# Seven products in the middle layer of two token blocks, with a given order for TensorE

## Chip, cores, metric

One Trainium2 chip, one core. The metric is the device time of one execution in microseconds (us). Every timed run has a state, fast or slow, by its time against the fastest of the same kernel; only fast runs enter a ratio.

## The reference

```python
# q, k, v: (8, 8, 576, 64); w_in: (512, 2048); w_out: (2048, 512); all float32
scores = q @ k.transpose(0, 1, 3, 2) / 8
ret = scores * Dmat                      # gamma_h ** (i - j) for i >= j, else 0
x = (ret @ v).transpose(0, 2, 1, 3).reshape(4608, 512)
h = x @ w_in
out = (h * cos(h)) @ w_out               # (4608, 512) float32
```

## The kernel before

PSUM, in banks, is where TensorE leaves its results; SBUF is where the other tiles stand. The tokens go through in nine blocks of 512, numbered from 0. Attention runs in "sessions" (64x64 matmuls) that end in an x tile `xt`. The middle layer makes h, the cosine and their product g (`gt`) in 16 tiles a block; the last layer multiplies g with `w_out`.

Middle layer, one tile: four matmuls, a cosine on ScalarE from PSUM, a multiply on VectorE (g multiply) from PSUM and SBUF.

```python
def mlp1(self, j, f, ses, prio):
    ...
    for c in range(4):
        inst = e.matmul(bank, WIN[c, f], xt[c], start=(c == 0), stop=(c == 3))   # 512 columns
    self.one("act", ..., e.activation(cb, bank, AF.Sin, bias=CPI))               # cos(h) = sin(h + pi/2)
    self.one("dve", ..., e.tensor_tensor(gt[f], bank, cb, ALU.mult))             # g = h cos(h)
```

Last layer of blocks 1 to 8: a 2x2 block product by seven products instead of eight. VectorE makes the operand sums (S sums, bf16); ScalarE copies a bank out in the middle of an accumulation (a snapshot), because products 1, 6, 7 and 4 accumulate in the same bank A; VectorE combines.

```python
def wino2(self, j, base, span):
    for q in range(2):                          # S1 .. S4: 128x1024 bf16 <- two SBUF inputs
        self.one("dve", 610, lambda e: e.tensor_tensor(sv(i, q), x(), y(), op), ..., port=True, name=f"S{i}_{j}")
    ...
    for n, p in enumerate((1, 2, 6, 5, 7, 3, 4)):
        ...                                     # two tasks of 8 matmuls, 256 columns each
        if p == 1: snap("p1", A)                # ScalarE copies the bank
        elif p == 2: comb(0, 0, Bb, "p1")       # VectorE: PSUM + SBUF -> SBUF, float32
        elif p == 6: snap("u2", A)
        ...
```

The order on every engine comes from a list scheduler that the program runs while it is being built. Operations marked `port` (elementwise work between SBUF tiles on VectorE or GpSimd) are kept apart in its reckoning.

```python
def pick(e):
    for t in ready[e]:
        s = max(free[e], est[t], a)
        if t.port:
            s = max(s, port_free["pool" if e == "dve" else "dve"])
        if t.ni:
            s = max(s, fetched(t))              # a model of instruction fetch, TensorE only
        cand.append((s, t))
    ...
```

GpSimd casts k (`natk`), scales v (`natv`) and most of q (`qnat`), and issues the weight loads.

## Time and profile before

| | before |
|---|---|
| timed, first comparison | 306.41, 306.94, 306.71 fast, 314.08 slow; mean of the fast 306.69 us |
| profiled run | 312.0 us (a slow one), span 310.3 |
| TensorE, VectorE, ScalarE, GpSimd busy | 95, 66, 61, 35% |

### The profile page before, as it was taken

What the parts mean: (1) busy time and instruction counts of PE and PEld (TensorE: products, weight loads), DVE (VectorE), ACT (ScalarE), POOL (GpSimd) and SP (SyncE); (2) the same over time, 40 slices, a digit from 0 to 9 for tenths busy, and PEclk for the clock granted to TensorE, in tenths of its full rate; (3) what the DMA queues carried; (4) which work ended last, traced back from release to release, by engine and by line L of the source; (5) the groups of instructions that cost most, each with busy time, mean ns of one, the idle gap of its engine ahead of it and who ended that gap; (6) DMA issues with size and microseconds to landing.
All of it is one profiled execution on the core that took longest, in us unless ns stands there. A gap on an engine that the chain in (4) does not pass through costs nothing.

```text
span 310.3 us, 10091 instructions
## 1 busy us (share of the span) xinstructions
PE 294.1 (95%) x4274; PEld 214.7 (69%) x4277; DVE 206.3 (66%) x371; ACT 188.3 (61%) x340; POOL 108.9 (35%) x134
## 2 busy tenths in 40 slices
PE   8987999799889999999998799999999999999995
PEld 8866755688778888567855375768656666666684
DVE  3574973475984769898478487775769667666641
ACT  3476843888959775856373566474686665455430
POOL 2261058759517581931362631312741000000000
PEclk9999999999999999999999799999999999999999
DMA  9999999999977999894999749269701100300123
GB/s 172 222 159 206 205 229 217 253 270 219 219 157 189 122 204 285 159 171 109 234 219 247 181 48 235 61 114 195 161 13 72 70 2 0 127 10 2 63 76 136
DMA packets 126397, 46.80 MB, mean 151 GB/s; under 512 B 105104, under 2 KB 122000, under 8 KB 126352
## 3 DMA queue, kind: packets, MB, share of 16 engines
q1 hardware_dynamic: 122128, 41.95, 63.3%
q0 software_dynamic: 4224, 4.19, 8.4%
q8 instruction: 34, 0.56, 0.8%
q14 instruction: 11, 0.09, 0.1%
HBM read 36.70 MB, written 9.44 MB: 149 GB/s over the span
## 4 chain that ended last, share of the span: by engine, by line
PE 87%; DVE 3%; ACT 3%; issue 2%; DMA 2%; POOL 2%; DVEq 0%
PE bk L763 39%; PE bk L886 32%; PE bk L800 4%; PE bk L418 2%; DMA stgq<-in_q_dram 2%; PE bk L661 2%; PE bk L652 2%; PE bk L634 2%; PE st L643 2%; PE bk L575 2%; DVE gt L774 1%; PE bk L593 1%; DVE pt L723 1%; POOL win L743 1%; POOL wout L747 1%
## 5 line engine op out<-in xcount | busy, mean ns | idle before, releaser
L774 DVE TENSOR_TENSOR gt<-bk,cb 128x256 bf16<-128x256 f32 (+1 forms) x192 | 103.7, 555 | 59.5 <-ACT cb L771 52.9
L763 PE MATMUL bk<-xt,win 128*128 128x256 bf16 (+1 forms) x768 | 140.1, 327 | 2.3 <-issue 1.3
L771 ACT ACTIVATE cb<-bk,cpi 128x256 bf16<-128x256 f32 (+1 forms) x192 | 108.4, 585 | 55.6 <-PE bk L763 54.0
L763 PEld LDWEIGHTS bk<-xt,win 128*128 128x128 bf16 x768 | 72.9, 98 | 44.0 <-issue 2.3
L512 POOL TENSOR_TENSOR natv<-stgv,wv 128x512 bf16<-128x512 f32 x38 | 41.3, 1097 | 36.1 <-DMA stgv<-in_v_dram 23.3
L477 POOL CAST natk<-stgk 128x512 bf16<-128x512 f32 x36 | 22.0, 626 | 62.0 <-DMA stgk<-in_k_dram 34.6
L557 POOL TENSOR_TENSOR qnat<-stgq,wq 128x512 bf16<-128x512 f32 x36 | 38.6, 1092 | 13.5 <-DMA stgq<-in_q_dram 5.9
L723 DVE TENSOR_TENSOR pt<-bk,tri 128x512 bf16<-128x512 f32 (+1 forms) x46 | 29.6, 683 | 14.8 <-PE st L643 12.8
L476 ACT ACTIVATE sbd<-st 128x512 bf16<-128x512 f32 x32 | 19.3, 603 | 22.6 <-PE st L643 22.4
L886 PE MATMUL bk<-wout,s 128*128 128x256 bf16 x256 | 32.2, 273 | 0.0
L886 PE MATMUL bk<-tw,s 128*128 128x256 bf16 x256 | 31.6, 273 | 0.5 <-DVE s L847 0.5
L886 PE MATMUL bk<-wout,gt 128*128 128x256 bf16 x256 | 31.6, 273 | 0.0
L886 PEld LDWEIGHTS bk<-wout,s 128*128 128x128 bf16 x256 | 24.7, 98 | 6.6
L886 PEld LDWEIGHTS bk<-tw,s 128*128 128x128 bf16 x256 | 24.6, 98 | 6.1 <-DVE s L847 0.8
L886 PEld LDWEIGHTS bk<-wout,gt 128*128 128x128 bf16 x256 | 24.7, 98 | 4.6 <-DVE pt L723 0.2
L476 ACT ACTIVATE sn<-bk 128x512 f32<-128x512 f32 x24 | 14.4, 604 | 18.7 <-PE bk L886 18.7
L476 ACT ACTIVATE xt<-bk 128x512 bf16<-128x512 f32 x36 | 23.1, 694 | 0.3 <-PE bk L661 0.2
L898 DVE TENSOR_TENSOR os<-bk,sn 128x512 f32<-128x512 f32 x24 | 16.4, 685 | 8.2 <-PE bk L886 8.2
L886 PE MATMUL bk<-tw,gt 128*128 128x256 bf16 x128 | 17.3, 282 | 0.0
L886 PEld LDWEIGHTS bk<-tw,gt 128*128 128x128 bf16 x128 | 12.9, 101 | 4.2 <-issue 0.6
L418 PE MATMUL bk<-one 128*128 128x128 bf16 x181 | 14.3, 244 | 1.1 <-DVE lq L441 1.1
L800 PE MATMUL bk<-wout,gt 128*128 128x512 bf16 x61 | 14.8, 379 | 0.2
(63 smaller groups left out, 230.7 us busy)
## 6 DMA issues: line engine op xcount, KB each, us to landing
stgk<-in_k_dram SPq DMA_DIRECT2D x32, 256.0 KB, 5.0
stgv<-in_v_dram SPq DMA_DIRECT2D x32, 256.0 KB, 5.4
out_dram<-os SPq DMA_DIRECT2D x15, 512.0 KB, 3.5
stgq<-in_q_dram SPq DMA_DIRECT2D x12, 512.0 KB, 7.0
stgq<-in_q_dram SPq DMA_DIRECT2D x8, 256.0 KB, 4.9
win<-in_moe_w_in_dram POOLq DMA_DIRECT2D x4, 512.0 KB, 7.6
wout<-in_moe_w_out_dram POOLq DMA_DIRECT2D x4, 512.0 KB, 14.7
out_dram<-os SPq DMA_DIRECT2D x6, 256.0 KB, 3.5
```

The lines of the kernel that those rows point to most:

```text
L418: inst = e.matmul(ap(self.at(self.wb), 512, 0, 128, 0, [1, 128]), self.ONE.ap(), self.ONE.ap(), start=True, stop=True, skip_group_check=True)
L476: return self.one(eng, dur, lambda e: e.activation(dst(), src(), AF.Copy), r=r, w=w, **kw)
L477: return self.one(eng, dur, lambda e: e.tensor_copy(dst(), src()), r=r, w=w, port=True, **kw)
L512: self.one(ve, vd, lambda e, b2=b2: e.tensor_tensor(ap(self.at(t["natv"]), 1024, 0, 128, 512 * b2, [D, H], [1, D]), ap(self.at(t["stgv"]), ...
L557: self.one("dve" if fast else "pool", 620 if fast else 990, lambda e, t=t, y=y: e.tensor_tensor(ap(self.at(t["qnat"]), 1024, 0, 128, y * 5 ...
L723: self.one("dve", 610, lambda e, hp=hp: e.tensor_tensor(ap(self.at(pt), 1024, p0, n, 512 * hp, [64, 8], [1, 64]), ap(self.at(sc[hp]), 512, ...
L763: inst = e.matmul(ap(self.at(bk), 512, 0, 128, 0, [1, n]), ap(self.WIN, 4 * DFF, 0, 128, c * DFF + 128 * f, [1, 128]), ap(self.at(xt), 204 ...
L771: self.one("act", 70 + n, lambda e: e.activation(ap(self.at(cb), TB, 0, 128, 0, [1, n]), ap(self.at(bk), 512, 0, 128, 0, [1, n]), AF.Sin, ...
L774: self.one("dve", 75 + n / 0.96, lambda e: e.tensor_tensor(ap(self.at(gt), NF * TB, 0, 128, f * TB + 256 * h0, [1, n]), ap(self.at(bk), 51 ...
L800: inst = e.matmul(self.at(bk).ap(), ap(self.at(gt), NF * TB, 0, 128, f * TB + 256 * half + 128 * tt, [1, 128]), ap(self.WOUT, NF * DM, 0, ...
L886: inst = e.matmul(ap(self.at(bank), 512, 0, 128, 256 * tt, [1, 256]), l(f, tt), rr(f), start=(first and f == 0 and tt == 0), stop=True, sk ...
L898: self.one("dve", 610, lambda e: e.tensor_tensor(view(h, c), ap(self.at(bank), 512, 0, 128, 0, [256, 2], [1, 256]), ap(self.at(sn[name]), ...
```

## The change

Its intent: save TensorE's streaming in the middle layer of blocks 7 and 8 by seven products there too; give TensorE's order as a list found beforehand, with the other engines scheduled around it; make the start shorter.

```diff
+    SEVEN = 7
+    ORDER = [int(x) for x in """2 0 1 3 4 10 5 6 ... 409 410 411""".split()]   # 412 TensorE tasks (cut)
+    FIRST = [(0, "v", 0), (1, "q", 1)]
-    NOXBAR = set(range(7))
+    NOXBAR = set(range(8))
@@ Prog.add: also an engine's own earlier reads are waited for
-            deps += [d for d in readers if d.eng != eng or d.sem or sem]
+            deps += [d for d in readers if d.eng != "pe" or eng != "pe"]
@@ Graph.run: fetch model and priority rule for TensorE go
+                if e == "pe" and t.idx != first:
+                    continue
@@ weight sums, once, 8 of 128x1024 bf16
+    def win_sums(self):
+        ...
+                self.one("pool", 2100, lambda e, dst=dst, x=x, y=y: e.tensor_tensor(dst(), x(), y(), ALU.subtract),
+                         r=r, w=[w], port=True, late=4000)
@@ operand sums of x, 4 of 128x512 bf16 a block
+    def xsums(self, j):
+            self.one("dve", 340, lambda e, ...: e.tensor_tensor(v(i), x(), y(), op), ..., port=True, name=f"X{i}_{j}")
@@ seven products M1 .. M7 for each of 4 groups a block
+    def mlp1w(self, j, g, base, span):
+        for n, p in enumerate((1, 2, 6, 5, 7, 3, 4)):
+            ...                               # 4 matmuls of 256 columns; snapshots on ScalarE, combines on VectorE
+            eng = "dve" if bank else "pool"   # 12 of 16 g multiplies a block on GpSimd, from SBUF
+            self.one(eng, 608 if eng == "dve" else 1000, lambda e: e.tensor_tensor(out(h, n), h_tile, cb, ALU.mult), ...)
@@ graph
+            if j + 1 == self.SEVEN:
+                tiles([X(15), Y(15), X(17), Y(17)])
+                self.win_sums()
+            if not last and j + 1 >= self.SEVEN:
+                self.xsums(j + 1)
+                for g in range(4):
+                    self.mlp1w(j + 1, g, base + PER * g / 4, PER / 4)
... (cut: the filler count, bookkeeping of buffers, the gates of the weight loads)
```

`NOXBAR` names the tiles that TensorE transposes, not a DMA; both traces have 16 DMA transposes, so it changes nothing here. Fillers are matmuls on constants at the start whose result nobody uses.

## The prediction

> **What bounds the kernel now.** I read the page first (busy shares, chain that ended last), then the same chain in order of time, TensorE's waits, busy time by stage, the groups by shape, and last the timeline of the first 25 us.
>
> ```profile
> span 310.3 us, 10091 instructions
> ...
> PE 294.1 (95%) x4274; PEld 214.7 (69%) x4277; DVE 206.3 (66%) x371; ACT 188.3 (61%) x340; POOL 108.9 (35%) x134
> ...
> PE 87%; DVE 3%; ACT 3%; issue 2%; DMA 2%; POOL 2%; DVEq 0%
> ```
>
> TensorE is busy 95% of the span and holds 87% of the last chain; VectorE and ScalarE have a third of the span free. So time is TensorE's own streaming, plus its waits. The chain in order of time gives both streaming rates (start us, us, what):
>
> ```profile
> 11.67 6.10 DMA stgq<-in_q_dram
> 18.07 2.30 POOL win L743 x3
> 20.36 2.22 POOL wout L747 x3
> 22.59 1.08 POOL natv L512
> ...
> 126.15 8.63 PE bk L763 x40
> ...
> 169.47 3.28 issue
> ...
> 293.95 13.12 PE bk L886 x120
> ```
>
> 40 matmuls of 512 columns in 8.63 us are 216 ns each; 120 of 256 columns in 13.12 us are 109 ns each. A middle-layer tile over a whole block (4 x 216) costs 0.86 us, half a product of the last layer (8 x 109) 0.87 us. The first four lines are the start: a query load, then six weight-load issues on GpSimd, then the value scaling that the y session waits for.
>
> TensorE's waits (engine, line, waited for: us, times, longest):
>
> ```profile
> PE st L643 <- issue: 3.3, 1, 3.3
> PE bk L634 <- POOL natv L512: 1.8, 1, 1.8
> PE bk L763 <- issue: 1.3, 1, 1.3
> ...
> PE bk L575 <- DVE gt L774: 1.0, 1, 1.0
> PE bk L763 <- ACT xt L476: 0.8, 1, 0.8
> ```
>
> The largest does not belong to the timed runs, I think. Busy time by stage, around it (PE, PEld, DVE, ACT, POOL, then granted clock, DMA share, GB/s):
>
> ```profile
> 125.00:169.20 44.20, 44.20 (x562) 28.91 (x561) 33.95 (x50) 26.46 (x42) 20.74 (x22) 1.00 0.89 189
> 169.20:177.00 7.80, 4.52 (x79) 2.55 (x70) 3.23 (x6) 3.32 (x6) 3.88 (x5) 0.78 0.93 239
> ```
>
> The stall, and half clock for about 3.4 us behind it, cost about 3.4 + 1.7 = 5.1 us. The profiled execution took 312.0 us, the timed median is 306.71: 5.3 us less. So a timed run probably has neither, and on the profile's axis its TensorE ends at 307.1 - 5.2 = 301.9 us. From 123 us to the end it then has no wait worth naming.
>
> **What the skill says.** "TensorE: Matmul & The Clock Gate", Back-to-back issue gap, gives N/2.4 + 2.5 ns for an isolated warm matmul: 109 and 216 ns for 256 and 512 columns, which is what the chain shows (its lower 131 ns at N=512 with weight loads is not seen here). Same page, What's actually happening: the clock halves after about 3.4 us idle; the 3.3 us stall with clock 0.78 behind it agrees. "Runtime: NRT & Kernel Launch", Instruction fetch mechanics: instructions stream in blocks of 256 by a DMA queue, the crossing "mostly hidden". The page counts 34 instruction packets on one queue, and the two issue waits (1.3 and 3.3 us) look like such fetches come late behind data. "GPSIMD Engine Reference", Elementwise, has GpSimd 1.96 times slower than VectorE at tensor_tensor; here it is less, 1095 against 685 ns for 128x512.
>
> **The change, part by part.**
>
> *Seven products for the middle layer of blocks 7 and 8* (numbered from 0). Removed: 16 tiles of 4 matmuls at 512 columns per block, 64 x 216 ns = 13.8 us. Added: 4 groups x 7 products x 4 matmuls at 256 columns, 112 x 109 ns = 12.2 us. Saved on TensorE: 1.6 us a block, 3.2 us for two, where TensorE sets the time. Around it:
>
> ```profile
> L771 ACT ACTIVATE cb<-bk,cpi 128x512 bf16<-128x512 f32 x96 | 66.1, 688 | 44.6 <-PE bk L763 44.4
> L774 DVE TENSOR_TENSOR gt<-bk,cb 128x512 bf16<-128x512 f32 x96 | 65.2, 689 | 37.0 <-ACT cb L771 33.5 <-PE bk L763 3.0
> ...
> L512 POOL TENSOR_TENSOR natv<-stgv,wv 128x512 bf16<-128x512 f32 x38 | 41.3, 1097 | 36.1 <-DMA stgv<-in_v_dram 23.3 <-PE bk L661 12.3
> ...
> L898 DVE TENSOR_TENSOR os<-bk,sn 128x512 f32<-128x512 f32 x24 | 16.4, 685 | 8.2 <-PE bk L886 8.2
> ...
> L476 ACT ACTIVATE sn<-bk 128x512 f32<-128x512 f32 x24 | 14.4, 604 | 18.7 <-PE bk L886 18.7
> ```
>
> A block's group has 3 snapshots more on ScalarE: 12 x 604 = 7.2 us a block. VectorE's 16 multiplies of 689 ns become 12 combines of 685 and 4 multiplies, so the same, plus 4 operand sums of about 0.4. GpSimd, idle from 240 us on before, takes 12 multiplies a block of about 1.1 us and once eight weight sums of 128x1024, which I estimate at 2.2 us each by doubling its 1097 ns: 44 us in all. A late block has 12.2 us of middle and 12.2 us of last layer on TensorE, 24.4 us; ScalarE's 11.0 + 7.2 + 2.4 = 20.6 us (Sin, snapshots, the last layer's copies) and VectorE's 11.0 + 1.6 + 6.1 + 2.1 = 20.8 us (combines and multiplies, operand sums, the last layer's sums and combines) stay below, at 85%. They fit but have little slack left: bank A is snapshotted between products 1, 6 and 7, and drain 0.2 + copy 0.6 + signal 0.05 us is covered only by two products of 0.44 us between. In most groups the order has those two; in one (block 7, third group) product 6 follows product 1 directly: 0.85 us lost.
>
> *The given order.* TensorE's waits of the 24 to 125 us stretch, from start-to-start times against the usual of each task: 0.9 and 0.3 before the x2/x3 session, 0.9 for xt behind it, 0.4, 0.6 + 0.4 behind the x4 session, 0.7 (a sum S1), 0.3, 0.2, 0.1: 4.9 us, besides the 1.5 of an issue wait at 28 us. In the changed order I measured the same way how much TensorE work lies between each producer and its consumer. It puts output tiles of the last layer between the x2/x3 tasks (-1.2), seven middle tiles before y2/y3 (-0.4) and an earlier last tile before S1 (-0.5). It keeps the xt wait (0.9; the middle layer still follows its session directly), about 0.7 around the x4 session, and gains new ones: 0.45 before session 12/13 (its bank is left by a tile issued 0.87 us before; chain 0.2 + 0.69 + 0.69 + signals), 0.85 as above, some 0.3 in small ones. These come to 3.2 us; before, the same arithmetic gave 2.4 where the trace had 4.9, because engines also queue. I take 4.0. So order: -0.9.
>
> *Start, fillers.* The fillers are not fewer in the built program: 184 against 181, but 29 instead of 71 stand before the first transpose, which before was ready by 4.6 us and ran at 7.5:
>
> ```profile
> 1.13 6.55 PE L418 MATMUL bk<-one 128*128 128x128 bf16 x71 [1.13 <-DVE lq L441]
> 7.51 0.39 PE L575 MATMUL bk<-idn,natk 128*128 128x128 bf16 x4
> ```
>
> The transposed query copy, and the second query's scaling queued behind it on VectorE (10.9 us), come some 2 us earlier, and so does the 11.67 us load in the chain. DMA is busy there, so I count 0.9 us of it at the y session, of which 0.44 goes back: one middle tile fewer stands before that session. Net -0.5.
>
> *Tail.* One product of block 7 now fills a wait near the end, so its store of 512 KB goes out beside the last ones: +0.3.
>
> Sum: -3.2 - 0.9 - 0.5 + 0.3 = -4.3; 306.7 - 4.3 = 302.4 us, 1.4% faster.
>
> **Rivals.** *Nothing is left of the seven products:* copies and combines in chains with no slack give 0.3 us in each of 8 groups back, 2.4 us, and the time is near 305. For it: ScalarE and VectorE at 85%, thin spacing. Against: the order was chosen around just these. *Order pays in full:* waits of 1.5 us in place of 4.9, and 1.6 us at the start, make it 306.7 - 3.2 - 3.4 - 1.6 + 0.3 = 298.8. For it: every wait of before sits at a place that a list can repair. Against: the xt wait and the one after product 1 stand in the new list. *Fetch:* the order rule that looked at instruction fetch is gone and there are about 200 TensorE instructions more; one stall as at 169 us in timed runs would be 3 to 5 us: 306. For it: it happened in the profiled run even with the rule. Against: most dense stretches (sessions) are spaced as before.
>
> **Range and chances.** The spread is +-1.5 from the order, +-1 from the start, +-1.5 from the late blocks, upward also a fetch: 299.0 to 305.8. Faster by over 2% needs under 300.6, a gain of 6.1, which the second rival alone reaches: 0.25. Within 2%: 0.72. Slower: 0.03.
>
> **What would show it.** Middle-layer products at 109 ns each and 24.4 us of them; the first transpose near 4.6 us and the y session near 23 us instead of 23.8; TensorE's waits for ScalarE snapshots and VectorE combines in the last 90 us under 2 us in total; GpSimd busy there. I am wrong if that stretch shows waits of several us, if GpSimd's weight sums are waited for, if issue waits are new, or if the early stretch has lost its waits altogether.

## More of the kernel before

The prediction shows the lines on TensorE. Two more matter later. First, the stages after 228 us (columns: stage, length, busy time and instructions of PE, PEld, DVE, ACT, POOL, then granted clock, DMA share, GB/s):

```profile
228.00:256.00 28.00, 28.00 (x410) 17.76 (x409) 21.86 (x34) 19.63 (x34) 2.08 (x2) 1.00 0.11 40
256.00:300.00 44.00, 43.94 (x338) 30.35 (x337) 29.49 (x45) 20.96 (x32) 0.00 (x0) 1.00 0.13 49
```

TensorE is idle for 0.06 of these 72 us, and GpSimd (fifth pair) has nearly nothing to do. Second, VectorE's S sums of the same stretch (228 to 303 us; line, engine, out<-in, shapes, count | busy us, mean ns | idle before):

```profile
L847 DVE TENSOR_TENSOR s<-s,gt 128x1024 bf16<-128x1024 bf16 x6 | 4.7, 780 | 0.2
L853 DVE TENSOR_TENSOR s<-gt,s 128x1024 bf16<-128x1024 bf16 x6 | 4.1, 687 | 0.1
```

About 690 ns is what such a sum takes when GpSimd is idle; the 780 is taken up again below.

## The result, and the profile after

The changed kernel took 318.46, 317.65 and 316.71 us in fast runs (mean 317.61) and 321.96 in a slow one; it is correct. Ratios here are the mean of one kernel's fast runs over the mean of the other's fast runs of the same rounds, so not quite the ratio of the medians: 317.61 / 306.69 = 1.036, with a 95% interval of 1.031 to 1.040. It is slower by 3.6%, outside the predicted range. The profiled run is a fast one (318.46 us).

From the page of the changed kernel, busy shares and the chain that ended last:

```profile
PE 294.9 (93%) x4376; PEld 223.8 (71%) x4376; DVE 216.4 (68%) x379; ACT 199.2 (63%) x364; POOL 154.7 (49%) x166
...
PE 78%; DVE 7%; ACT 6%; DMA 4%; issue 2%; POOL 2%; POOLq 1%; DVEq 0%
```

TensorE's share of the chain fell from 87 to 78%; VectorE's and ScalarE's rose from 3% each to 7 and 6%. GpSimd's busy time rose by 46 us. TensorE's busy time did not fall, although there is less to stream: part of it ran at half clock. The stages tell where (columns as above):

```profile
169.00:186.00 17.00, 14.98 (x202) 9.04 (x200) 15.14 (x22) 10.18 (x18) 8.45 (x7) 0.90 1.05 232
228.00:256.00 28.00, 24.04 (x416) 17.56 (x415) 21.13 (x28) 16.27 (x31) 15.75 (x11) 0.94 0.11 40
256.00:300.00 44.00, 42.46 (x496) 36.27 (x495) 35.02 (x50) 33.87 (x59) 25.66 (x22) 1.00 0.07 26
```

From 228 to 256 us TensorE is idle for 4 of 28 us and the clock is 0.94, where before it had not a gap. TensorE's waits (engine, line, waited for: us, times, longest):

```profile
PE bk L647 <- DVE gt L787: 3.2, 2, 2.0
PE bk L901 <- DVE s L828: 2.2, 1, 2.2
...
PE bk L901 <- DVE stgq L891: 0.8, 1, 0.8
PE bk L901 <- ACT stgv L489: 0.7, 1, 0.7
```

L647 is a session: it waited 2.0 us at 177 us (2.4 us by start-to-start times, which is the figure used further below) and 1.2 us at 240 us for a bank that VectorE's g multiply was to leave. L901 are the seven products; the largest of their waits is for an operand sum of x. Here is that one, in the timelines of VectorE, GpSimd and TensorE (start us, us, engine, line, out<-in, count):

```profile
243.48 0.82 DVE L992 TENSOR_TENSOR s<-gt 128x1024 bf16<-128x1024 bf16 x1
244.22 3.52 DVE L828 TENSOR_TENSOR s<-xt 128x512 bf16<-128x512 bf16 x2
247.66 0.41 DVE L828 TENSOR_TENSOR s<-s,xt 128x512 bf16<-128x512 bf16 x1
...
243.70 2.58 POOL L809 TENSOR_TENSOR stgk<-win,stgk 128x1024 bf16<-128x1024 bf16 x1
246.24 1.22 POOL L525 TENSOR_TENSOR natv<-stgv,wv 128x512 bf16<-128x512 f32 x1
...
248.13 1.21 PE L901 MATMUL bk<-s,stgk 128*128 128x256 bf16 x6 [2.17 <-DVE s L828]
```

Two x sums took 3.52 us together. The third, with GpSimd idle, took 0.41. The first ended 0.28 us after GpSimd's weight sum had ended, the second 0.28 us after GpSimd's scaling of v, and TensorE's next product waited 2.17 us. Behind this wait, and behind that at 177 us, the granted clock was half for 3.4 us (columns of the stages):

```profile
180.20:183.60 3.40, 3.40 (x88) 2.61 (x74) 3.40 (x5) 2.84 (x5) 1.24 (x1) 0.50 1.16 152
248.40:251.80 3.40, 3.40 (x19) 2.44 (x17) 2.19 (x5) 1.60 (x3) 0.00 (x0) 0.50 0.02 5
```

A product's four matmuls took 0.85 us there instead of 0.44, so each of these stretches cost about 1.7 us. The holding shows as well in the means of VectorE's sums from 228 to 303 us (columns as above):

```profile
L998 DVE TENSOR_TENSOR s<-gt,s 128x1024 bf16<-128x1024 bf16 x5 | 6.8, 1367 | 0.1
L828 DVE TENSOR_TENSOR s<-xt 128x512 bf16<-128x512 bf16 x4 | 5.8, 1484 | 0.7 <-ACT xt L489 0.7
```

### What TensorE lost, by stage

To compare kernels with different work and order, I gave each of TensorE's tasks (a tile, half a product, a session) the shortest start-to-start time that its kind has in any of the traces (the lowest tenth, where there are over 30 of a kind). The sum is the work; what a stretch took above its work is lost: waits, half clock and the fill at the start. Stages end at the amount of work that the kernel before had done at 53, 125, 186 and 228 us. This is my reckoning from the traces, one profiled run per kernel. Stretches of half clock come early in some runs and not in others (list_only at 71.6 us, later_dve at 21.0 and 72.2 us), so in the first two columns differences of 1 or 2 us say little. All values are us; the rows below the second belong to the experiments.

| kernel | work | to 53 | 53-125 | 125-186 | 186-228 | after 228 | TensorE ends |
|---|---|---|---|---|---|---|---|
| before | 270.8 | 23.0 | 6.7 | 5.6 | 0.4 | 0.6 | 307.1 |
| changed | 267.6 | 24.5 | 5.8 | 4.1 | 0.8 | 10.0 | 312.8 |
| list_only | 270.8 | 24.1 | 8.4 | 2.8 | 0.8 | 1.5 | 308.5 |
| seven_greedy | 267.6 | 23.0 | 7.2 | 5.0 | 0.4 | 4.4 | 307.6 |
| sums_on_dve | 267.6 | 23.5 | 6.1 | 2.6 | 0.8 | 4.3 | 304.9 |
| session_later | 267.6 | 23.5 | 5.0 | 3.1 | 0.8 | 12.5 | 312.3 |
| later_dve | 267.6 | 25.0 | 8.5 | 3.5 | 0.9 | 4.2 | 309.7 |
| short_scales | 267.6 | 24.4 | 6.0 | 1.1 | 0.8 | 4.8 | 304.7 |
| short_late | 267.6 | 23.3 | 6.0 | 2.7 | 0.8 | 3.3 | 303.6 |
| short_both | 267.6 | 23.1 | 7.0 | 1.1 | 0.8 | 2.5 | 302.1 |
| late_gaps | 267.6 | 24.2 | 8.6 | 4.3 | 0.8 | 3.9 | 309.3 |
| late_gaps2 | 267.6 | 23.2 | 9.0 | 2.9 | 0.8 | 2.8 | 306.3 |
| short_gaps | 267.6 | 24.4 | 7.5 | 1.1 | 0.8 | 2.3 | 303.7 |
| greedy_dve | 267.6 | 22.3 | 6.1 | 5.8 | 2.3 | 2.0 | 306.0 |
| greedy_block8 | 269.2 | 22.9 | 6.7 | 0.6 | 0.4 | 2.2 | 302.1 |
| before_held | 270.8 | 23.0 | 7.4 | 6.0 | 0.8 | 1.1 | 309.1 |
| old_war | 267.6 | 23.4 | 7.1 | 3.0 | 0.8 | 10.0 | 311.8 |

The 5.6 of the kernel before from 125 to 186 us is nearly all the stall at 169 us that the prediction describes; greedy_block8, with the same order up to there, had none in its profile and lost 0.6. That stall comes and goes: with it, the four profiled runs of this early order took 311.1 to 314.0 us, without it the one took 307.0. So a run of the kernel before without it would end TensorE at 307.1 - 5.0 = 302.1 us, and against that the changed kernel is 10.7 us later: 3.2 less work, 1.5 more lost up to 53 us, 0.8 less up to 125, 3.5 more from 125 to 186, 0.3 more up to 228, and 9.4 more after 228. From TensorE's end to the end of the span it is 3.6 us against 3.3.

### The profile page after: what moved, and what is told of

Its sections match the earlier page's. It is cut to its first block, busy times and chain, and to the rows that moved or that the text cites. A ratio compares the mean times of both kernels' runs of the same rounds, so it can differ in the third digit from the quotient of the medians.

```text
span 316.4 us, 10344 instructions
## 1 busy us (share of the span) xinstructions
PE 294.9 (93%) x4376; PEld 223.8 (71%) x4376; DVE 216.4 (68%) x379; ACT 199.2 (63%) x364; POOL 154.7 (49%) x166
## 4 chain that ended last, share of the span: by engine, by line
PE 78%; DVE 7%; ACT 6%; DMA 4%; issue 2%; POOL 2%; POOLq 1%; DVEq 0%
PE bk L776 29%; PE bk L1031 28%; PE bk L901 8%; PE bk L945 4%; DMA stgq<-in_q_dram 3%; PE bk L647 2%; PE bk L665 2%; DVE gt L787 2%; PE bk L674 2%; PE st L656 2%; DVE s L992 2%; PE bk L588 1%; ACT cb L784 1%; DVE s L828 1%; PE bk L431 1%
## 5 line engine op out<-in xcount | busy, mean ns | idle before, releaser
L787 DVE TENSOR_TENSOR gt<-bk,cb 128x256 bf16<-128x256 f32 (+1 forms) x160 | 81.7, 528 | 48.7 <-ACT cb L784 42.7
L776 PE MATMUL bk<-xt,win 128*128 128x256 bf16 (+1 forms) x640 | 107.4, 315 | 4.0 <-DVE pt L736 1.7
L784 ACT ACTIVATE cb<-bk,cpi 128x256 bf16<-128x256 f32 (+1 forms) x160 | 85.5, 563 | 38.6 <-PE bk L776 35.7
L776 PEld LDWEIGHTS bk<-xt,win 128*128 128x128 bf16 x640 | 60.0, 98 | 36.8 <-DVE pt L736 2.3
L525 POOL TENSOR_TENSOR natv<-stgv,wv 128x512 bf16<-128x512 f32 x38 | 42.1, 1119 | 23.7 <-PE bk L674 17.7
L570 POOL TENSOR_TENSOR qnat<-stgq,wq 128x512 bf16<-128x512 f32 x36 | 37.8, 1068 | 17.3 <-DMA stgq<-in_q_dram 8.3
L1031 PE MATMUL bk<-wout,gt 128*128 128x256 bf16 x256 | 33.6, 279 | 0.0
L884 POOL TENSOR_TENSOR gt<-stgv,cb 128x512 bf16<-128x512 f32 x16 | 19.2, 1204 | 24.5 <-ACT cb L880 14.5
L1031 PEld LDWEIGHTS bk<-tw,s 128*128 128x128 bf16 x256 | 24.5, 99 | 5.7 <-DVE s L992 1.0
L489 ACT ACTIVATE xt<-bk 128x512 bf16<-128x512 f32 x36 | 23.2, 693 | 0.9 <-PE bk L674 0.9
L489 ACT ACTIVATE kt<-bk 128x512 bf16<-128x512 bf16 x20 | 12.0, 600 | 11.9 <-PE bk L588 11.2
L1031 PE MATMUL bk<-tw,gt 128*128 128x256 bf16 x128 | 16.1, 273 | 0.0
```

Of the source, the lines that this page charges most:

```text
L489: return self.one(eng, dur, lambda e: e.activation(dst(), src(), AF.Copy), r=r, w=w, **kw)
L525: self.one(ve, vd, lambda e, b2=b2: e.tensor_tensor(ap(self.at(t["natv"]), 1024, 0, 128, 512 * b2, [D, H], [1, D]), ap(self.at(t["stgv"]), ...
L570: self.one("dve" if fast else "pool", 620 if fast else 990, lambda e, t=t, y=y: e.tensor_tensor(ap(self.at(t["qnat"]), 1024, 0, 128, y * 5 ...
L776: inst = e.matmul(ap(self.at(bk), 512, 0, 128, 0, [1, n]), ap(self.WIN, 4 * DFF, 0, 128, c * DFF + 128 * f, [1, 128]), ap(self.at(xt), 204 ...
L784: self.one("act", 70 + n, lambda e: e.activation(ap(self.at(cb), TB, 0, 128, 0, [1, n]), ap(self.at(bk), 512, 0, 128, 0, [1, n]), AF.Sin, ...
L787: self.one("dve", 75 + n / 0.96, lambda e: e.tensor_tensor(ap(self.at(gt), NF * TB, 0, 128, f * TB + 256 * h0, [1, n]), ap(self.at(bk), 51 ...
```

## The experiments

The theory to be tested (theory 1 in the expectations): VectorE's sums of two SBUF tiles are held while GpSimd works, VectorE works in order, so what TensorE waits for comes late. Rivals: the given list itself, the seven products' chains and load, the new same-engine waits. The scatter is large: the same kernel before took 306.4 to 313.6 us in 36 runs. So I read verdicts under 1% from the table of stages, not from the times alone.

### pairs: the disputed cost by itself

A kernel of its own; the output is zeros. Eight VectorE operations of one kind run beside a stream of GpSimd operations of one kind, one combination after another.

```diff
+for v in (None, "ssum", "xsum", "gmul", "comb"):        # VectorE's operations of the changed kernel
+    for a in (None, "cast", "scale", "mult", "wsum"):   # GpSimd's operations of the changed kernel
+        ...                                             # both start together, after the pair before
```

> The disputed cost by itself: four VectorE operations of the changed kernel (S sum, 128x1024 bf16 from two SBUF tiles; x sum, 128x512 bf16 from two SBUF tiles; the g multiply, 128x512 from PSUM and SBUF; the combine, 128x512 float32 from PSUM and SBUF), eight of each, alone and beside four GpSimd operations of the changed kernel (natk's cast, natv's scaling, the g multiply, a weight sum). The output is zeros on purpose. Theory 1 (VectorE's sums of two SBUF tiles are held while GpSimd works): S sums about 680 ns alone and 1.3 us or more beside GpSimd's scaling, multiply or weight sum, x sums 410 ns alone and 1.2 us or more beside them, while the two operations that read PSUM stay at 680 to 690 ns within 10%. Rival (no such coupling, VectorE is late for another reason): every VectorE operation within 10% of its time alone, beside anything.

Measured, in a single run (VectorE's rows; the name says operation and neighbour, so `dssumscale` is S sums beside scalings):

```profile
L118 DVE TENSOR_TENSOR dssumwsum<-gtin 128x1024 bf16<-128x1024 bf16 x8 | 18.3, 2362 | 7.7 <-POOL pmultssum L135 7.7
...
L118 DVE TENSOR_TENSOR dssummult<-gtin 128x1024 bf16<-128x1024 bf16 x8 | 11.6, 1518 | 7.9 <-POOL pscalessum L132 7.9
L118 DVE TENSOR_TENSOR dssumscale<-gtin 128x1024 bf16<-128x1024 bf16 x8 | 10.8, 1421 | 10.5 <-POOL pcastssum L130 10.5
...
L118 DVE TENSOR_TENSOR dssumnone<-gtin 128x1024 bf16<-128x1024 bf16 x8 | 4.9, 685 | 62.1 <-POOL pwsumnone L137 62.1
...
L124 DVE TENSOR_TENSOR dgmulwsum<-bk,cb 128x512 bf16<-128x512 f32 x8 | 4.9, 680 | 10.8 <-POOL pmultgmul L135 10.8
```

An S sum takes 685 ns alone, 1041 beside casts, 1421 beside scalings, 1518 beside multiplies and 2362 beside weight sums; an x sum 416 alone, 1154 beside scalings (a little under the 1.2 us that I had written), 1250 beside multiplies and 2094 beside weight sums. The g multiply and the combine, which read one operand from PSUM, take 679 to 681 ns beside anything. GpSimd is slowed in return: a weight sum beside S sums 2567 instead of 2115 ns, a cast about 1070 instead of 613 while S sums run, and unchanged beside the two that read PSUM. In the trace the two engines take turns, one operation each: beside weight sums every S sum but the first lasts 2.60 us, and a pair takes 2.52 us, which is 2115 + 685 less 0.28 that overlap. The rival falls; the cost is real. What it adds to a VectorE sum is about the length of the GpSimd operation, whatever the length of the sum: beside weight sums of 2.1 us it is 1.9 us, to S sums (0.685 to 2.60 us) and to x sums (0.416 to 2.33 us) alike.

### list_only and seven_greedy: each half of the change alone

```diff
 list_only (from the changed kernel)
-    SEVEN = 7
+    SEVEN = 9                    # the 28 M tasks of each block replaced in the list by its 16 direct tiles
 seven_greedy (from the kernel before)
+    win_sums, xsums, mlp1w as in the change, the new rule of same-engine waits; no list, scheduler as before
```

> The changed kernel without its seven products in the middle layer: the given list kept, each block's 28 M tasks replaced in place by the 16 direct tasks of the kernel before. Theory 1 (VectorE's sums held by GpSimd's work, at the places where the list puts a wait right behind): the waits at 177 us (2.4 us and 1.2 us of half clock after) do not hang on the seven products and stay, those after 228 us (about 9 us with their half clock) go, so about 310 to 311 us, 1.0 to 1.4% over before. Rival A (the list itself costs it all): 316 us or more. Rival B (seven products cost it all): 306 to 307 us, as before.

> The kernel before, its own scheduler making the order, with the seven products of blocks 7 and 8 added; no given list, same-engine waits as in the changed kernel. Theory 1: the waits near GpSimd's weight sums and multiplies are there with any order, because the scheduler's model knows of no held VectorE sum longer than its own port rule: 308 to 314 us, and no wait at 177 us. Rival A (the given list is at fault, the seven products are sound): 303 to 304 us, below before. Rival B (the scheduler's choice cannot place seven products at all): 318 us or more.

list_only took 312.4 us median, 1.013 of before (1.007 to 1.019), a little above the 310 to 311 that I had written, with a stretch of half clock at 71.6 us in its trace; it lost 1.5 us after 228 us, and kept the wait before the session x12y11/x13y12 (2.0 us). seven_greedy took 308.19 and 308.82 us in its fast runs, 1.000 of before (0.992 to 1.009), with 4.4 us lost after 228 us. So neither half makes 10 us of loss there: 1.5 and 4.4 become 10.0 only together. The seven products saved 3.2 us of work in seven_greedy and gave it all back. (Its profiled run is a slow one, with the stall at 169 us; the loss after 228 us lies behind that.)

### sums_on_dve: GpSimd's weight sums moved away

```diff
-                self.one("pool", 2100, lambda e, dst=dst, x=x, y=y: e.tensor_tensor(dst(), x(), y(), ALU.subtract),
+                self.one("dve", 610, lambda e, dst=dst, x=x, y=y: e.tensor_tensor(dst(), x(), y(), ALU.subtract),
```

> The changed kernel with its eight weight sums on VectorE instead of GpSimd; nothing else. Theory 1: at 240 us (1.2 us) and 245 us (2.2 us and 1.7 to 1.9 us of half clock) VectorE's sums were slow only beside GpSimd's weight sums of 2.1 to 2.6 us each; without them these waits go and VectorE gets 8 sums of 0.7 us, 5.5 us, more work in a stretch where it has that much slack: about 313 us, 1.4 to 1.7% under the changed kernel. Rival (VectorE's load of 85% there is what makes TensorE wait): the 5.5 us on VectorE make it no faster or slower, 318 us or more.

310.4 to 312.4 us in fast runs, 1.015 of before (1.006 to 1.023) against 1.036: as theory 1 had it, and a little better than the 313 us that I had written. The waits at 240 and 245 us went; the loss after 228 us fell from 10.0 to 4.3, although VectorE had 5.5 us more to do. VectorE's load alone is not what made TensorE wait.

### session_later and later_dve: the list's order at 177 us

```diff
 ORDER (entries are numbers of tasks; here by name)
- ... m1_4_14  P2_4  sesx12y11/x13y12  P1_4  P2_4  m1_5_3 ...
+ ... m1_4_14  P2_4  P1_4  P2_4  sesx12y11/x13y12  m1_5_3 ...
 later_dve: this and the edit of sums_on_dve
```

> The changed kernel with one entry of the given list moved: the session x12y11/x13y12 two places later, behind P1_4 and P2_4. Theory 1 in its form for 177 us (the list puts a session whose bank VectorE's g multiplies must free right behind them, and VectorE's S sums stand in front of these, held by GpSimd): 1.7 us of other work fits into the wait, so of 2.4 us at most 0.7 is left and the 1.2 us of half clock after it goes: 1.7 to 3 us less than the changed kernel, about 315 to 316 us. Rival (VectorE is late by itself, so the next task that needs it waits instead): as the changed kernel, 318 us.

> Both edits at once: the weight sums on VectorE and the session two places later. Theory 1: the two gains add up, about 6 us and 2 to 3 us: 309 to 310 us, within 1% of before, still not under it, since the thin chains at 263, 297 and 302 us (0.9, 0.9 and 0.6 us) and the longer tail stay. Rival (the waits move on to the next place where VectorE is late): no better than the weight sums on VectorE alone, 312 us.

Both missed. session_later took 317.9 to 321.9 us; later_dve took 311.8 to 315.3 us, no better than sums_on_dve. The trace of session_later shows why at 177 us (start us, us, engine, line, out<-in, count, idle time before and what ended it):

```profile
177.15 1.05 PE L1034 MATMUL bk<-wout,gt 128*128 128x256 bf16 x8 [0.73 <-DVE gt L790]
...
181.06 3.19 PE L779 MATMUL bk<-xt,win 128*128 128x512 bf16 x14 [1.67 <-ACT xt L492]
```

The session itself (from 178.12 us) no longer waited. Half a product ahead of it waited 0.7 us for a g tile of VectorE. The larger wait, 1.7 us, is one that my edit made: the two half products that I put before the session had stood behind it, and had covered the time in which ScalarE copies the session's x tile for the first middle tile of block 5. later_dve has this wait too (1.7 us). From 125 to 186 us session_later lost 3.1 us instead of 4.1. After 228 us it lost 12.5 instead of 10.0, 3.7 of them in one wait for an S sum. So these two runs do not show whether another order could cover the wait at 177 us; the next experiment takes that wait away without touching the order.

### short_scales, short_late, short_both: GpSimd's operations shortened

These give wrong results. Nothing changes but the number of columns that GpSimd works on, an eighth; the order and the dependences stay, and the products that would read weight sums read another tile of the same size.

```diff
 short_scales: scalings of v and q in the second half of the batches
-   [D, H], [1, D]     (64 of each 64 columns)
+   [D, H], [1, 8]     (8 of each 64)
 short_late: weight sums and GpSimd's g multiplies
-   [DFF, 2], [1, 512]        [256, 2], [1, 256]
+   [DFF, 2], [1, 64]         [256, 2], [1, 32]
 short_both: both; (in all three the cosine's argument is scaled down to stay in range)
```

> Wrong on purpose: the changed kernel with GpSimd's scalings of q and v, for all tiles of the second half of the batches (from about 120 us on), done on 8 of each 64 columns, so that each takes some 0.2 us in place of 1.1 us; everything else is left in place (the cosine's argument is scaled to zero so that the wrong values stay in its range). Theory 1: with nothing of GpSimd's in the way VectorE's four or five S sums before the session at 177 us take 0.7 us each, not 0.93 to 1.5 us, about 2.5 us sooner, and the 2.4 us wait there and its half clock go: 3 to 4 us under the changed kernel, 314 to 315 us; the waits at 240 and 245 us stay. Rival (the wait is VectorE's load or the list alone): the wait at 177 us stays, 318 us.

> Wrong on purpose: the changed kernel with GpSimd's weight sums and g multiplies done on an eighth of their columns, so 0.2 to 0.3 us each in place of 2.1 and 1.2 us; VectorE, ScalarE and TensorE do what they did. Theory 1: the waits at 240 us (1.2), 245 us (2.2 and 1.7 of half clock), 297 us (0.9) and 302 us (0.6) go, about 6.5 us under the changed kernel: 311 to 312 us; the waits at 177 us and at 263 us (a chain through ScalarE) stay. Rival (the seven products' chains through ScalarE and VectorE, and their load, make the waits): 1 us at the most, 317 us.

> Wrong on purpose, both shortenings at once: GpSimd's scalings from the second half of the batches on, its weight sums and its g multiplies on an eighth of their columns. It closes the sum. Theory 1 (the GpSimd operations that hold VectorE's sums cost about 7 us; what is left over the prediction is the thin chain at 263 us and the start): the waits at 177, 240, 245, 297 and 302 us all go, TensorE ends at 302 to 303 us, and the time is 307 to 308.5 us, 10 us under the changed kernel and still not the 302.4 predicted. Rival (the two shortenings take the same wait away, so they don't add up): no better than the better of the two alone, 309.5 us.

short_scales took 310.4 to 311.4 us, short_late 309.1 to 310.7 (I had written 311 to 312), short_both 306.83 to 310.01 in fast runs, against 316.7 to 318.5 of the changed kernel in the first comparison. In short_scales the wait at 177 us fell from 2.4 us to 0.7 and the loss from 125 to 186 us from 4.1 to 1.1; it also took away most of the late waits (4.8 us lost after 228 us), where I had written that they would stay, since a scaling of v stood in the 3.52 us shown above. In short_late the S sums after 228 us were back at 0.70 us and the x sums at 0.42:

```profile
L1001 DVE TENSOR_TENSOR s<-gt,s 128x1024 bf16<-128x1024 bf16 x6 | 4.2, 704 | 0.1
...
L829 DVE TENSOR_TENSOR s<-xt 128x512 bf16<-128x512 bf16 x4 | 1.5, 420 | 0.7 <-ACT xt L489 0.7
```

By the table short_both ends TensorE at 302.1 us, 10.6 before the changed kernel, with the same work, list and load on VectorE, ScalarE and TensorE: 3.0 of it from 125 to 186 us and 7.5 after 228. That is the holding of VectorE by GpSimd, with the half clock behind its waits. The shortenings also give GpSimd's own results sooner, but that is little: among the changed kernel's waits after 26 us TensorE has none for GpSimd, and VectorE's S sums waited 0.5 us for its g tiles after 228 us. short_both is level with the kernel before (1.004, interval 0.999 to 1.010), not below it. By the table, against a kernel before without its stall, the 3.2 us saved go again: 0.4 up to 125 us, 0.9 from there to 228, 1.9 after.

### before_held: the holding alone, in the kernel before

```diff
+        if i % 4 != 3:                       # 12 multiplies of 128x512 in blocks 7 and 8 each
+            self.one("pool", 1000, ... e.tensor_tensor(dummy, float32 tile, bf16 tile, ALU.mult), r=[g tile i], ...)
+        if j + 1 == 7 and i < 8:             # 8 sums of 128x1024 bf16
+            self.one("pool", 2100, ... e.tensor_tensor(dummy, bf16 tile, bf16 tile, ALU.subtract), r=[g tile i], ...)
```

> The kernel before with GpSimd work added whose result nobody uses: 8 sums of 128x1024 bf16 and 24 multiplies of 128x512, as many and as long as the changed kernel's, from 243 us on, each released by one g tile of blocks 7 and 8. TensorE's order differs in 4 of 388 places, VectorE's in 9 of 344. Theory 1 in its full form (holding alone is enough): VectorE's S sums after 243 us go from 0.69 us to 1.2 us or more each, some 24 of them, 12 us more in a stretch where VectorE is idle for 20 of 72 us, and TensorE loses 2 us or more after 228 us against 0.5: 309 us or more for the fast runs. Theory 2 (holding needs the seven products' fuller VectorE and their chains): the S sums are held as much, but the slack takes it up, TensorE loses less than 1 us there and the fast runs stay at 306.5 to 307.5 us.

Theory 2 of this text came nearer. The S sums of the kernel before were held at least as much as in the changed one (228 to 303 us):

```profile
L862 DVE TENSOR_TENSOR s<-s,gt 128x1024 bf16<-128x1024 bf16 x6 | 7.5, 1252 | 0.2
...
L868 DVE TENSOR_TENSOR s<-gt,s 128x1024 bf16<-128x1024 bf16 x6 | 6.6, 1106 | 0.1
```

and yet TensorE lost 1.1 us after 228 us instead of 0.6; the fast runs are at 0.999 of before (0.991 to 1.008). They took 308.4 to 310.8 us, more than the 306.5 to 307.5 that I had written, but the kernel before took 307.3 to 311.6 in the same call. Nor is a fuller VectorE enough to make holding cost time (columns of the stages):

```profile
256.00:300.00 44.00, 43.94 (x335) 29.95 (x333) 38.83 (x45) 21.93 (x34) 39.40 (x27) 1.00 0.13 49
```

VectorE was busy for 38.8 of 44 us here, in the changed kernel for 35.0, and still TensorE was idle for only 0.06 us. I read this so: holding costs time where a product needs its operand sum, bank or combine within a task or two. That is argued from the waits of the changed kernel; no run varies the distance alone.

### late_gaps, late_gaps2, short_gaps: the thin chains

```diff
 late_gaps (with the weight sums on VectorE), by task name
- M1_7_2 M6_7_2 M2_7_2 M5_7_2 M7_7_2        M4_8_3 P1_8 P3_7 P5_8 P6_8 ... P4_7
+ M1_7_2 M2_7_2 M5_7_2 M6_7_2 M7_7_2        P1_8 P3_7 M4_8_3 P5_8 P4_7 P6_8 ...
 late_gaps2
- P7_6 M1_7_2 M6_7_2                        M4_8_3 P1_8 P3_7 P5_8 P6_8 P6_8 P2_8 ... P4_7
+ M1_7_2 P7_6 M6_7_2                        P1_8 P3_7 M4_8_3 P5_8 P4_7 P6_8 P2_8 P6_8 ...
 short_gaps: the order of late_gaps2 in short_both
```

> The weight sums on VectorE, and four entries of the given list moved at the three late gaps: M6_7_2 two places later, behind M2_7_2 and M5_7_2; P1_8 and P3_7 ahead of M4_8_3; P4_7 ahead of P6_8. Theory 1 with its rest (0.85, 0.93 and 0.63 us are chains through ScalarE and VectorE with too little work put between): the three gaps fill, 2.0 to 2.4 us under the weight sums on VectorE alone (312.0), so 309.5 to 310 us. Rival (VectorE's load is the bound there and the wait only moves): less than 0.8 us, 311.2 us or more.

> The weight sums on VectorE, and the late gaps filled as the chains ask: P7_6 between M1_7_2 and M6_7_2; P1_8 and P3_7 ahead of M4_8_3; P4_7 ahead of the first P6_8 and P2_8 ahead of the second. Theory 1: what TensorE loses after 228 us falls from 4.3 to 2.3 us or less, and no task there is over 0.4 us late; the time follows within the scatter of the start, 309 to 311.5 us. Rival (the waits move to the next task each time): 3.8 us or more are still lost there, as in the first attempt.

> Wrong on purpose: GpSimd's scalings, weight sums and multiplies shortened as before, with the late gaps filled as in late_gaps2. If holding and the thin chains are all that stood between the change and its intent, TensorE loses 1.5 us or less after 228 us, ends at 301 us, and the fast runs take 305 to 307 us, at or just below the kernel before: what is still short of the 302.4 predicted is the start and the early order, which gave nothing. If something else holds the late stretch, 308 us as without the gaps filled.

late_gaps missed: three of its six runs were slow, the fast ones took 308.6 to 312.0 us (1.012 of before, 1.004 to 1.019), and 3.9 us were lost after 228 in the profiled run (a slow one), hardly less than the 4.3 of sums_on_dve. The 0.85 us behind M1_7_2 had only become 0.90 behind M6_7_2, because my edit put M7 directly behind M6, and M7 waits for M6's snapshot as M6 for M1's. With P7_6 between (late_gaps2) that gap and the two near the end went; a new one of 0.6 us came at the last session, and the loss fell to 2.8 us, not to the 2.3 that I had written. The fast runs took 310.3 to 312.7 us, 1.005 of before (0.998 to 1.012). short_gaps, expected at 305 to 307 us, took 308.8 us: 2.3 us lost after 228, hardly less than short_both and more than the 1.5 that I had written, and 1.8 more than short_both up to 125 us. Its ratio, 0.996 (0.990 to 1.003), says nothing against a before that was itself scattered. So some 2 us of the late loss, in pieces of 0.1 to 0.6 us, stay with the seven products and this list even without holding.

### greedy_dve and greedy_block8: towards a better version

```diff
 greedy_dve: seven_greedy with the weight sums on VectorE (as in sums_on_dve)
 greedy_block8: seven_greedy with
-    SEVEN = 7
+    SEVEN = 8
```

> The kernel before with its own scheduler and the seven products in blocks 7 and 8, the weight sums on VectorE. With the weight sums on GpSimd TensorE lost 4.3 us after 228 us, against 0.5 in the kernel before. Theory 1: without GpSimd's sums of 2.1 us about 1 to 2 us of that goes: 306 to 307.5 us, 0 to 0.5% under the kernel before. Rival (VectorE's load): 309 us or more.

> The kernel before with its own scheduler and the seven products in block 8 alone, the weight sums on GpSimd. It saves half, 1.6 us of products. Theory 1: GpSimd's 12 multiplies and 8 sums still meet VectorE's sums of one block instead of two, TensorE loses about half of 4.3 us after 228 us: no gain, 306.5 to 308 us, within 0.3% of before. Rival (the chains of block 7 beside the sessions of the last tiles make the loss): 305.5 us or less.

greedy_dve lost 2.0 us after 228, but 2.3 instead of 0.4 from 186 to 228 us, where four of the eight sums now stand on VectorE; the longest wait of TensorE there, 1.0 us, is for a copy of k on ScalarE, and that the sums brought it about is not shown. Its fast runs took 307.73, 308.58 and 311.1 us, the ratio is 1.006 (0.999 to 1.013): no gain, where I had written 306 to 307.5. greedy_block8 saved 1.6 us of work and lost 1.6 more after 228, as I had expected: its stall-free run took 307.00, beside 306.45 as the best of before in the same call; the other three fast runs, 310.5 to 311.3 us, lie above the 306.5 to 308 that I had written; ratio 1.009 (1.002 to 1.016). No version of mine beats the kernel before.

### old_war: the rule of same-engine waits

```diff
-            deps += [d for d in readers if d.eng != "pe" or eng != "pe"]
+            deps += [d for d in readers if d.eng != eng or d.sem or sem or eng == "pool"]
```

> The changed kernel with the rule of before for waits of an engine on its own earlier reads, except on GpSimd, where the check does not allow it. Theory 1: these waits are for operations long done, so nothing changes beyond the scatter: 317 to 319 us. Rival (the new waits slow VectorE or ScalarE): 315 us or less.

315.4 to 317.7 us in fast runs, and the loss after 228 us is 10.0 again, with the same waits (2.2, 0.8 and 0.7 us for seven products). The new rule on VectorE and ScalarE is not the cause. On GpSimd the old rule can't be tried: the check before the chip then finds a race there, between a read of a raw k tile and a weight sum's later write into its buffer.

## Why the prediction was wrong, point by point

It had given "slower" a chance of 0.03. Of its own signs of being wrong, the first came: waits of several us in the late stretch. Its products did run at about 109 ns a matmul at full clock, and the first transpose came at 4.72 us as it said.

- **Seven products, -3.2 us: right as work.** The table has 270.8 against 267.6 us.
- **"They fit but have little slack left": this step failed.** The sum of VectorE's work took the operand sums of x at about 0.4 us and the S sums at 0.76 (6.1 us for eight), their mean in the kernel before, while the same paragraph moved 44 us of work to GpSimd in the same stretch. There the x sums that were held took 0.97 to 2.34 us each, S sums 1.37 on average in one group. Adding up durations measured beside an almost idle neighbour was the mistake; with the order's short distances behind such sums it became 10.0 us of loss after 228 us, of which short_both takes 7.5 away. The trace could have warned: the 780 ns of the kernel before in the row shown above is five sums of 0.69 us and one of 1.22, at 233.7 us, and that one ran beside a scaling of q on GpSimd. Plainer still, two sums of `w_out` of the same shape took 2.90 us in that trace beside two scalings of v (start us, us, engine, line, out<-in, count):

```profile
51.70 2.90 DVE L826 TENSOR_TENSOR wout<-wout 128x1024 bf16<-128x1024 bf16 x2 [6.25 <-PE bk L800]
...
51.56 2.49 POOL L512 TENSOR_TENSOR natv<-stgv,wv 128x512 bf16<-128x512 f32 x2
```

  The program says it too: `pick` above lets, in its reckoning, no `port` operation of VectorE start before GpSimd's last one has ended. And the page that answers it was not opened: the Trainium skill, "SBUF — State Buffer", SBUF: two separate sides, says that VectorE and GpSimd share one port pair under "an **exclusive lock**, not a bandwidth split", for VectorE operations with two SBUF inputs among others, and that "the other fully blocks". pairs agrees: turns of one operation each (2.52 us a pair), and none of it for operations that read PSUM. I had cited only "GPSIMD Engine Reference", 3.1 Elementwise, for how slow GpSimd is; its 1. Specifications name the shared interfaces as well.
- **The given order, -0.9 us from waits of 4.9 that become 4.0: this term was mis-sized.** Up to 125 us the loss is 30.3 against 29.7 us, and over all rows of the table 31.0 us on average for the twelve kernels with the list against 29.7 for the five without, so nothing was gained. (The waits that the prediction lists there add up to 4.8, not 4.9.) "0.45 before session 12/13" was 2.4 us and some half clock behind it; after 228 us, where I had 1.2 us of waits, 10.0 us were lost. The 0.85 that it foresaw in block 7 is there, as a wait of 0.7 us for a snapshot. With GpSimd shortened the late loss is 2.5, so the list's spacing was nearer to what I had counted, for engines that keep their times.
- **Start, -0.5 us: wrong sign.** The query load was issued at 9.75 instead of 11.67 us, and landed no sooner. The chain of the changed kernel in order of time (start us, us, what):

```profile
9.75 8.29 DMA stgq<-in_q_dram
...
24.07 0.22 PE bk L647 x2
```

  It took 8.29 us where it took 6.10 before, and landed at 18.04 instead of 17.77: I take it that the transfers in front of it set when it comes. The y session began at 24.07 us; I had expected about 23, and it was 23.80 before. It is not one run's scatter: up to 53 us the twelve kernels with the list lost 23.1 to 25.0 us, the five without 22.3 to 23.0. I had counted half of the gain although I wrote that DMA is busy there.
- **The stall at 169 us "does not belong to the timed runs": half right.** By their times (306.4 to 306.9 us) the three fast runs of the first set do not have it, but runs of 311 to 314 us of the same early order come again and again, and the profiles of before, seven_greedy, greedy_dve and before_held (all with TensorE's order the same up to there) show it, as issue waits of 3.3, 2.7, 3.8 and 3.8 us; greedy_block8's, with that order too and at 307.0 us, does not. That it is instruction fetch stays unproved. The rival that blamed fetch for a loss falls for the profiled run of the changed kernel: no matmul there waits over 1.0 us on issue after 26 us, although the rule for it is gone.
- **The rival "nothing is left of the seven products" was nearest.** It put 2.4 us of chains against them; without holding (short_both) the loss after 228 us is 1.9 us above before. It had no term for holding.
- **Half clock after a wait** was in the prediction, for the stall of 3.3 us (the Trainium skill, "TensorE: Matmul & The Clock Gate", What's actually happening). It adds to the loss after shorter waits as well: behind the 2.2 us wait at 245 us the clock was half for 3.4 us, which cost another 1.7.

What stays open: which pieces make the last 2 us after 228 us; why the start with the list is about 1 us longer; whether another order could cover the wait at 177 us; and how often the stall at 169 us falls into a run.

## What to carry to other kernels

Before work is moved to GpSimd because it is idle, look at what VectorE does in the same stretch: VectorE's sums with two SBUF inputs then take turns with GpSimd, and each lasts longer by nearly the whole GpSimd operation (0.69 us became 2.60 beside one of 2.1), while operations that read one input from PSUM are not touched (0.68 us beside anything). Short GpSimd operations do less harm than long ones, and a sum that TensorE needs within a task or two must not meet one. Added cost on a side engine is free only while what follows it has slack: before_held made its S sums 1.7 times as long (0.69 to 1.20 us) and lost 0.5 us, the seven products with this list lost 9.

## What the Trainium skill lacked or had wrong

- "SBUF — State Buffer", SBUF: two separate sides: right on the exclusive lock and on its holding for whole instructions. It says that the one that starts first gets the ports, but not how two streams without gaps share them; here the two engines took turns strictly, and a pair took the sum of both times alone less 0.28 us (2115 + 685 ns gave 2.52 us; 613 + 685 gave 1.01 us).
- "GPSIMD Engine Reference", 3.1 Elementwise: its comparison of the engines (1.96 times slower) is of one instruction by itself. What the two cost each other has no figure there: a VectorE sum of 685 ns took 1041 to 2362 ns beside GpSimd, and GpSimd's weight sum 2567 instead of 2115 ns, which decides whether moving work pays.
- "TensorE: Matmul & The Clock Gate", What's actually happening: the clock halves after an idle window of about 3.4 us, by the page. Here waits of 2.02 and 2.17 us were each followed by 3.4 us at half clock (from 180.2 and from 248.4 us), so a wait well below 3.4 us can be enough; it need not be: behind old_war's wait of 2.15 us at 178 us the clock stayed full.
- No page that I read has the stall of 2.7 to 3.8 us at one and the same place of a program, which some runs show and others of the same order do not.
